# Gated attention with a low-rank mixer: rank sums in four parts, the 64-row tile's products on column halves, the opening's panels in order of use

## The chip, the cores and the metric

The kernel runs on one core of a Trainium2 chip. The metric is the device time of one execution in microseconds. Before the change the median of 11 runs is 1012.69 us (1009.78 to 1018.38).

## The reference

There are 8 batches of 3136 rows. Attention comes first, without a softmax; then a mixer, which adds a low-rank mix over the rows and a two-layer product over the channels:

```
scores = (z @ z.T) / 3136            # z: 3136 x 64; scores are symmetric
x      = u * (max(scores, 0)**2 @ v) # u, v: 3136 x 256
h      = (x.T @ U) @ V               # U: 3136 x 32, V: 32 x 3136
y      = x + h.T
out    = y + max(y @ w_ch1, 0) @ w_ch2   # 256 -> 1024 -> 256
```

Inputs and output are float32; the kernel multiplies in bf16 and sums in float32.

## The kernel before, in words

The rows are cut into 25 tiles: 24 of 128 rows (row index p*24 + t, so a tile is a stride over the rows) and tile 24, called NF, of 64 rows. The tiles are taken in the order 12, 13, ..., 24, 0, ..., 11 (`turns`). NT is 25, FIRST is 12, LEAD is 16, NG is 4.

**Scores.** Row panel j of the squared scores lies in A[j] and covers tiles j to j+12 (cyclically), 13 blocks of 128 columns. `score` (L298) makes a piece with two matmuls over 64 rows, one in each row half of the array; ScalarE applies ReLU and scale out of PSUM (L311), VectorE squares in place (L313). Scores are symmetric, so the blocks that tile o needs from the other 12 panels are the transpose of its own panel: SyncE's queue sends a DMA transpose into a strip (`turn`, L333). There are five strip buffers. `block` gives either a piece of A or of a strip.

**Attention.** `attend_steps` sums, for output tile o, 25 blocks of scores times v. Each block is split in two row halves (`half`, L371), which go to two PSUM banks; tiles go in pairs that share the two banks. `close_pair` adds the halves (ScalarE copy L385, VectorE add L386) and multiplies by u (L395), which gives x. Tile NF uses quarters (`quarter`, L405). There are two sets of two banks; `spare()` is the set that the open pair doesn't hold, or the one closed last where no pair is open. The scores of later panels are strewn between the attention's matmuls by `_spread`; the tables `own_at`, `first_at` and `next_at` say in which turn i of the loop each panel is made, and `turn(b, turns(i + AHEAD))` at the end of a turn transposes four tiles ahead.

**Mixer.** It lags a batch behind. `rank` (L462) sums x.T @ U over the tiles with U as the 32-column stationary operand, in all four 32-column groups of the array; every tile's product is made twice, so that groups 0 and 1 together hold the sum, and groups 2 and 3 hold it again. ScalarE casts the 128x256 result to t1_sb (L472). `low_rank` (L508, L522) multiplies by V over 64 rows and adds into x; then a DMA transpose (L481) makes ut. Chunks c of up to four tiles follow: `up_steps` (L540, ReLU in L558) makes the first products, `down_steps` (L582, L593) the second, adds x and stores. They run as bursts after turns 4, 8, 13 and 17, two chunks in each. Chunk 3 holds tiles NF, 0 and 1. First and second products of neighbouring chunks are interleaved evenly by `_merge`. With `alone`, every second step of first products uses the spare banks and splits its ReLU between VectorE and ScalarE; that is so for chunk 0.

**The end.** After the last batch's attention there come the last rank sum, in two parts with what is left of the batch before (the list `late`), then the last batch's own bursts with its low-rank products in them.

**The opening.** `start_up` computes tiles 12 to 15 with early scores, then tiles 16 to 19 from panels that are finished meanwhile: `rest` holds the missing parts of panels 8 to 15 (one block for panel 8, eight for panel 15), `more` the whole panels 20 to 23. Early loads go through GpSimd's queue, among them the first parts of the next batch's v. A tiny DMA into `mark` on SyncE's queue waits for the last of these parts, and so holds the first DMA transposes back until the loads have landed. The loop proper begins at turn 8, which is tile 20.

All engines follow the order in which the program is written out (the schedule is by hand), each with its own queue.

Of the kernel before, what the change touches and what calls it, by code (L numbers as in the profile page):

```python
# [7 lines left out]
FP32 = mybir.dt.float32  # L8
# [34 lines left out]
def kernel(  # L43
# [56 lines left out]
    def spare():  # L100

        return sets[(opened[0] + (0 if acc else 1)) % 2]
# [29 lines left out]
    def turns(i):  # L132
        return (FIRST + i) % NT
# [24 lines left out]
    def x_at(b, t, n=1):  # L158

        c, k = offset[t]  # L160
        return group(b, c)[:, :, k : k + n, :].rearrange("p a t c -> p t a c")
# [153 lines left out]
    def score_steps(b, j, k0=0, k1=NB):  # L315
        steps = []
        n = (k1 - k0) * P
        parts = _ceil_div(n, 1024)
        each = n // parts
        h = each // 2  # L320
        for i in range(parts):
            at = k0 * P + i * each

            def step(at=at):
                dst = A[j][:, at : at + each].rearrange("p (i h) -> p i h", i=2)
                score(b, [(j, j * P + at + i * h, h, dst) for i in range(2)])

            steps.append(step)
        return steps
# [124 lines left out]
    def rank(b, ps, n0=0, n1=NT):  # L454
# [17 lines left out]
        nc.scalar.copy(out=t1_sb, in_=ps[:, :D])  # L472
        t1[b] = t1_sb

    uT = {}

    def turn_x(b, c):
# [86 lines left out]
    def down_steps(b, c):  # L564
        pairs = []
        for t in chunks[c]:
            if pair_of(t)[0] == t:
                pairs.append([])
            pairs[-1].append(t)
        at = {}  # L570
        for t in chunks[c]:
            at[t] = sum(P if k < NF else TAIL for k in at)
        hold = {}

        def step(n, k):
            pair = pairs[n]
            if k == 0:
                hold[0] = spare()[1 - n]
            ps = hold[0]
            q = at[pair[k]]  # L580
            for ht in range(NH):
                mm(  # L582
                    out=ps[:, k * D : (k + 1) * D],
                    lhsT=relus[c][:, ht, q : q + P],
                    rhs=w2_bf[:, ht, :],
                    start=(ht == 0),
                    stop=(ht == NH - 1),
                )
            if k == len(pair) - 1:
                t, nk = pair[0], len(pair)  # L590
                o_sb = out_pool.tile([P, 2, D], FP32, name="o_sb")
                p = P if t < NF else TAIL
                nc.vector.tensor_tensor(  # L593
                    out=o_sb[:p, :nk, :].rearrange("p t (a c) -> p t a c", c=P),
                    in0=split(ps[:p, : nk * D]),
                    in1=x_at(b, t, nk)[:p],
                    op=ALU.add,
                )
                store = pool_dma if b + 1 < B else nc.sync.dma_start
                if t < NF:  # L600
                    store(out=rows(out[b])[:, t : t + nk, :], in_=o_sb[:, :nk, :])  # L601
                else:
                    store(out=out[b, NF * P :, :], in_=o_sb[:TAIL, 0, :])

        return [
            lambda n=n, k=k: step(n, k) for n in range(len(pairs)) for k in range(len(pairs[n]))
        ]

    def bursts_of(b):

        out_ = []
        for c in range(NC + 1):
            up = [lambda s=s, c=c: up_steps(c, c == 0)[s]() for s in range(NH // 2)] if c < NC else []
            down = down_steps(b, c - 1) if c else []
            out_.append((up, down))
        return out_
# [10 lines left out]
    def start_up():  # L627
# [26 lines left out]
            load_z(1, WHOLE)  # L654
        run(fetches)
        if B > 1:
            for part in V_PARTS[:4]:
                load_v(1, part)
        nxt = [s for j in range(LEAD, LEAD + NG) for s in turned(0, j)]
        rooms = [A[j % NT][:, : 2 * NG * P] for j in range(LEAD + NG, LEAD + 3 * NG)]  # L660
# [27 lines left out]
        for i, pair in enumerate(pairs):  # L688
            if i == 5 and B > 1:

                nc.sync.dma_start(out=mark, in_=v_both[1][:1, V_PARTS[3][1] - 1, :8])
            if i == 3:
                double_z(0, parts[2:])
            if i == 5:
                turn_on_pe([(16, NF)], [pair_psum().rearrange("p a w -> p (a w)")])
                turn_on_pe([(NF, NT)], [pair_psum()[:, 0, :]])
                extend_z(0)
            make(pair)
            if i > 5 and i % 2:
                nxt.pop(0)()  # L700
            if i > 1:
                use(pairs[i - 2], outs)
# [33 lines left out]
        ]  # L736
        run(_merge(nxt[2:], own))
        rest = []
        for j in range(FIRST - NG, LEAD):
            rest += score_steps(0, j, LEAD + NG - j, NB)  # L740
        more = [s for j in range(LEAD + NG, LEAD + 2 * NG) for s in score_steps(0, j)]
        for i, pair in enumerate(pairs):
            if i + 2 < len(pairs):
                make_stored(pairs[i + 2])
# [10 lines left out]
        for o in outs:  # L755
            js = [(o + 1 + i) % NT for i in range(HALF)]

            def close(o=o, j=js[-1]):
                beside(o, j, block(0, o, j), [o % 2 == 1] * 2)
                if o % 2:  # L760
                    close_pair(0, o)
                if o == outs[1]:
                    load_u(0, LEAD + NG)
                if o < outs[-1]:
                    turn(0, o + NG + 1)

            for i in range(3):
                some = js[4 * i : min(4 * i + 4, HALF - 1)]
                tail.append(lambda o=o, js=some: [beside(o, j, block(0, o, j)) for j in js])
            tail.append(close)  # L770
# [8 lines left out]
    for j, i in enumerate((6, 7, 8, 9, 3, 5, 4, 2, 9, 8, 7, 6)):  # L779
        own_at[i].append((j, 0, FIRST - j))  # L780

    first_at = {8: [(NT - 1, 0, NB), (0, 0, NB)], 9: [(1, 0, NB)], 10: [(2, 0, NB)]}
    first_at.update({11: [], 12: []})
    for j, i in zip(range(3, FIRST), (9, 10, 11, 11, 11, 12, 12, 12, 12)):
        first_at[i].append((j, 0, FIRST - j))

    next_at = {i: [] for i in range(NT)}
    for j in range(FIRST):
# [12 lines left out]
    for b in range(B):  # L801
        more = b + 1 < B
        begin = 0 if b else 2 * NG
        bursts = bursts_of(b - 1) if b else []
        burst_at = {4: (0, 1), 8: (2, 3), 13: (4, 5), 17: (6, 7)}
        own = own_at if b else first_at
        v_at = dict(zip((9, 12, 15, 18, 21), V_PARTS[4:]))
        ahead = dict(zip((2, 3, 6, 7, 10, 11, 14), range(NC)))
        for i in range(begin, NT):
            o = turns(i)  # L810
            fill = [s for key in own.get(i, ()) for s in score_steps(b, *key)]
            if more:
                fill += [s for key in next_at[i] for s in score_steps(b + 1, *key)]
                if b and i == 1:
                    load_z(b + 1, WHOLE)
                if b and i == 7:
                    turn_z(b + 1, ((FIRST, NF),))
                if b and i == 10:
                    turn_z(b + 1, ((0, FIRST),))
                if b == 0 and i in v_at:  # L820
                    load_v(b + 1, v_at[i])
                if i == 11:
                    extend_z(b + 1)
            main = attend_steps(b, o)
            if b and i in ahead:
                main.insert(17 if (i + (i > FIRST)) % 2 == 0 else 10, lambda c=ahead[i]: low_rank(b - 1, c))
            _spread(main, fill)
            if i + AHEAD < NT:
                turn(b, turns(i + AHEAD))
            elif more:  # L830
                turn(b + 1, turns(i + AHEAD - NT))
            elif i == NT - AHEAD:
                turn_x(b, 0)
            if b == 0 and i in puts:
                puts[i]()
            if b and i == 0:
                rank(b - 1, spare()[0])
            for n in burst_at.get(i, ()) if b else ():
                up, down = bursts[n]
                if not more and n >= NC - 1:  # L840
                    late += up + (down if n == NC else [])
                    up, down = [], (down if n < NC else [])
                steps = _merge(up, down)
                if more:
                    loads = [lambda k=k: load_v(b + 1, V_PARTS[k]) for k in ((n,) if n < NC else (n, n + 1))]
                    steps = _merge(steps, loads)
                    if n == 1:
                        for k, part in ((6, (FIRST, NF)), (3, (0, FIRST))):
                            steps.insert(k, lambda part=part: double_z(b + 1, (part,)))
                run(steps)  # L850
# [14 lines left out]
    for c in range(NC + 1):  # L865
        up, down = last[c]
        if c + 2 < NC:
            up.insert(3 if c == 0 else 1, lambda c=c: low_rank(b, c + 2, other))
        if c == 0:
            up.insert(1, lambda: low_rank(b, 0, other, False))  # L870
        run(_merge(up, down))

# [28 lines left out]
```

## Time and profile before

| | |
|---|---|
| median of 11 runs | 1012.69 us (1009.78 to 1018.38) |
| profiled execution | 1018.05 us, span 1016.3 us |
| TensorE busy | 992.1 us, 13823 matmuls |
| rank sums (L462) | 400 matmuls, 13.0 us |
| second products (L582) | 1600 matmuls, 204.7 us |
| granted TensorE clock | 0.998 |

Busy time is the union of an engine's instructions. A matmul's own duration includes its way through the array, and neighbours overlap; so what a group of matmuls costs is read from the start of the group to the start of the next. "Idle before, releaser" tells how long an engine waited before an instruction and what ended the wait.

### The profile page before, as it was taken

The numbers are of one execution on the slowest core, as the hardware profiler recorded it, in microseconds if no ns is written. First come the engines' busy times: TensorE is split into PE (matmuls) and PEld (weight loads), VectorE is DVE, ScalarE is ACT, GpSimd is POOL, SyncE is SP. The second block draws the span as 40 slices with busy tenths as digits, with TensorE's granted clock in tenths as the row PEclk, the third lists the DMA queues.
The fourth block names the chain that finished last, engine by engine and source line by source line (L and its number), as shares of the span: only waits on it lengthen the run. The fifth ranks groups of instructions, "written<-read, shape, count | busy, mean of one in ns | idle before, by whom it ended". The sixth has DMA issues, their size and how long they took to land.

```text
span 1016.3 us, 31322 instructions
## 1 busy us (share of the span) xinstructions
PE 992.1 (98%) x13823; PEld 784.9 (77%) x13863; DVE 540.0 (53%) x978; ACT 614.3 (60%) x835; POOL 171.7 (17%) x317
## 2 busy tenths in 40 slices
PE   8899999999999999899999999999999999999998
PEld 6678777887778877688787887778877788787866
DVE  6877654465445564346644556445664356542242
ACT  7977764576646675356764667556674666643154
POOL 5111112111121111121112211112111120011000
PEclk9999999999999999999999999999999999999999
DMA  9999989899898989989989999999989998667442
GB/s 186 198 212 184 181 130 206 170 175 156 184 170 168 184 152 150 172 170 174 162 174 168 182 167 147 186 167 172 174 153 194 167 184 143 141 145 168 105 97 95
DMA packets 414648, 167.97 MB, mean 165 GB/s; under 512 B 389472, under 2 KB 399136, under 8 KB 414512
## 3 DMA queue, kind: packets, MB, share of 16 engines
q1 hardware_dynamic: 385280, 99.68, 62.2%
q0 software_dynamic: 29232, 66.28, 28.2%
q8 instruction: 108, 1.77, 0.7%
q14 instruction: 28, 0.23, 0.1%
HBM read 61.88 MB, written 25.69 MB: 86 GB/s over the span
## 4 chain that ended last, share of the span: by engine, by line
PE 85%; DMA 6%; DVE 4%; ACT 2%; issue 1%; POOL 1%; SPq 0%; DVEq 0%; POOLq 0%; ACTq 0%
PE ps L371 44%; PE ps L582 16%; PE ps L540 16%; PE ps L298 6%; ACT A L311 2%; DMA strip<-A 2%; DMA out_dram<-o_sb 2%; DVE A L313 1%; PE ps L405 1%; PE ps L462 1%; DVE x_bf L522 1%; PE ps L508 1%; DMA z_c<-in_z_dram 1%; DMA ut<-x_bf 1%; DVE both L386 1%
## 5 line engine op out<-in xcount | busy, mean ns | idle before, releaser
L311 ACT ACTIVATE A<-ps 128x832 bf16<-128x832 f32 (+8 forms) x477 | 359.8, 769 | 153.0 <-PE ps L298 145.2
L371 PE MATMUL ps<-v,A 64*128 64x256 bf16 x4988 | 341.8, 269 | 4.6 <-DVE A L313 2.3
L313 DVE TENSOR_TENSOR A<-A 128x832 bf16<-128x832 bf16 (+8 forms) x477 | 244.9, 526 | 145.1 <-ACT A L311 141.8
L371 PE MATMUL ps<-v,strip 64*128 64x256 bf16 x4420 | 307.0, 269 | 1.4 <-DMA strip<-A 1.4
L371 PEld LDWEIGHTS <-A 64*128 64x128 bf16 x4988 | 244.8, 94 | 49.9 <-issue 14.0
L558 ACT ACTIVATE relu_bf<-ps 128x1024 bf16<-128x1024 f32 (+2 forms) x208 | 187.8, 909 | 143.6 <-PE ps L540 141.5
L371 PEld LDWEIGHTS <-strip 64*128 64x128 bf16 x4420 | 221.2, 94 | 36.0 <-DMA strip<-A 2.2
L593 DVE TENSOR_TENSOR o_sb<-ps,x_bf 128x512 f32<-128x512 f32 (+1 forms) x104 | 69.7, 670 | 254.5 <-PE ps L582 232.4
L582 PE MATMUL ps<-w_bf,relu_bf 128*128 128x256 bf16 x1600 | 204.7, 273 | 0.0
L540 PE MATMUL ps<-ut,w_bf 128*128 128x512 bf16 (+2 forms) x856 | 197.3, 351 | 3.5 <-DMA ut<-x_bf 1.0
L582 PEld LDWEIGHTS <-relu_bf 128*128 128x128 bf16 x1600 | 155.9, 98 | 47.0 <-issue 2.9
L540 PEld LDWEIGHTS <-w_bf 128*128 128x128 bf16 x896 | 85.0, 98 | 62.5 <-issue 6.2
L355 POOL DMA_DIRECT2D u_sb<-in_u_dram x96 | 53.6, 558 | 464.1 <-DVE x_bf L395 431.8
L298 PE MATMUL ps<-zT 64*128 64x416 bf16 (+8 forms) x812 | 130.7, 312 | 0.0
L385 ACT COPY both<-ps 128x512 f32<-128x512 f32 (+1 forms) x104 | 58.9, 566 | 80.8 <-PE ps L371 68.4
L601 POOL DMA_DIRECT2D out_dram<-o_sb x84 | 46.0, 548 | 278.1 <-DVE o_sb L593 274.7
L386 DVE TENSOR_TENSOR both<-ps,both 128x512 f32<-128x512 f32 (+1 forms) x104 | 69.2, 666 | 28.8 <-ACT both L385 28.5
L395 DVE TENSOR_TENSOR x_bf<-both,u_sb 128x512 bf16<-128x512 f32 (+1 forms) x104 | 69.8, 671 | 3.6
L522 DVE TENSOR_TENSOR x_bf<-ps,x_bf 128x512 bf16<-128x512 f32 (+1 forms) x112 | 65.4, 625 | 8.7 <-PE ps L508 8.7
L298 PEld LDWEIGHTS <-zT 64*128 64x128 bf16 x812 | 42.2, 94 | 4.0
L244 POOL DMA_DIRECT2D v<-in_v_dram x61 | 34.1, 561 | 2.0 <-DMA w_bf<-in_moe_w_ch_dram 1.0
L298 PE MATMUL ps<-relu_bf 64*128 64x416 bf16 (+9 forms) x121 | 21.9, 332 | 3.2 <-ACT A L311 2.5
(49 smaller groups left out, 209.6 us busy)
## 6 DMA issues: line engine op xcount, KB each, us to landing
u_sb<-in_u_dram POOLq DMA_DIRECT2D x96, 256.0 KB, 3.7
out_dram<-o_sb POOLq DMA_DIRECT2D x84, 256.0 KB, 3.1
v<-in_v_dram POOLq DMA_DIRECT2D x57, 192.0 KB, 4.7
strip<-A SPq DMA_TRANSPOSE x196, 5.5
out_dram<-o_sb SPq DMA_DIRECT2D x12, 256.0 KB, 2.0
z_c<-in_z_dram POOLq DMA_DIRECT2D x7, 384.0 KB, 5.5
u_sb<-in_u_dram POOLq DMA_DIRECT2D x16, 64.0 KB, 2.4
ut<-x_bf SPq DMA_TRANSPOSE x56, 3.5
```

Of the source, the lines that this page charges most:

```text
L298: mm(out=ps[:, k, :n], lhsT=zT[halves[k], j, :], rhs=zT_flat[halves[k], c : c + n], start=True, stop=True,)
L311: nc.scalar.activation(out=dst, in_=src, func=AF.Relu, scale=sc)
L313: nc.vector.tensor_tensor(out=dst, in0=dst, in1=dst, op=ALU.mult)
L371: mm(out=acc[t0][h][:, (o - t0) * D : (o - t0 + 1) * D], lhsT=w[halves[h]], rhs=v_both[b % 2][halves[h], j, :], start=start, stop=stop, **kw,)
L385: nc.scalar.copy(out=both[:, :w], in_=banks[1][:, :w])
L386: nc.vector.tensor_tensor(out=both[:, :w], in0=banks[0][:, :w], in1=both[:, :w], op=ALU.add)
L395: nc.vector.tensor_tensor(out=x_at(b, t0, n), in0=split(both[:, :w]), in1=u_sb[:, :n, :].rearrange("p t (a c) -> p t a c", c=P), op=ALU.mult,)
L522: nc.vector.tensor_tensor(out=q, in0=split(ps[h][:, : len(ks) * D]), in1=q, op=ALU.add)
L540: mm(out=ps[i][:, :w] if apart else ps[:, i, :w], lhsT=w1_bf[:, db, (hp + i) * P : (hp + i + 1) * P], rhs=uT[c][:, db, len(chunks[c]) * P ...
L558: nc.scalar.activation(out=relus[c][:, hp : hp + 2, :w], in_=ps[:, :, :w], func=AF.Relu)
L582: mm(out=ps[:, k * D : (k + 1) * D], lhsT=relus[c][:, ht, q : q + P], rhs=w2_bf[:, ht, :], start=(ht == 0), stop=(ht == NH - 1),)
L593: nc.vector.tensor_tensor(out=o_sb[:p, :nk, :].rearrange("p t (a c) -> p t a c", c=P), in0=split(ps[:p, : nk * D]), in1=x_at(b, t, nk)[:p] ...
```

## The change

The rank sum of batches 0 to 6 is formed once: every tile's product goes into one of four column groups in turn, so that each group holds a quarter of the sum. ScalarE copies the four parts to a float32 buffer, and VectorE adds the two row halves crosswise, so that both halves hold the same pair of sums as before. The last batch keeps `rank`.

The second products of tile NF use 64 columns instead of a 128-column window of which half was not used; the eight blocks of the sum alternate between the array's column halves, and VectorE adds the two results. In the bursts this tile's second product is taken first, ahead of the interleaving.

In the opening, the panels 15 to 8 of `rest` come in descending order; panel 23 is made in turn 8, and the panels of tiles 24, 1, 2 and 3 each a turn later than before, with those of 4 to 11 partly moved as well; the transposes of tiles 23, 24 and 0 follow in turns 8 and 9. Three parts of v instead of four are loaded early, and `mark` waits for the third.

At the end, chunk 6 of the batch before the last is also treated as `alone`, and the last batch's first low-rank product takes the set of banks that `spare()` gives.

```diff
+    def rank_once(b, ps):
+        for m in range(NT):
+            g = m % G
+            mm(
+                out=ps[g * R : (g + 1) * R, :D],
+                lhsT=U_bf[:, turns(m), :],
+                rhs=x_at(b, turns(m))[:, 0],
+                start=(m < G),
+                stop=(m + G >= NT),
+            )
+        t1_sb = small.tile([P, D], BF16, name="t1_sb")
+        sums = both_pool.tile([P, 512], FP32, name="both")
+        nc.scalar.copy(out=sums[:, :D], in_=ps[:, :D])
+        for h in range(2):
+            nc.vector.tensor_tensor(
+                out=t1_sb[halves[h], :],
+                in0=ps[halves[h], :D],
+                in1=sums[halves[1 - h], :D],
+                op=ALU.add,
+            )
+        t1[b] = t1_sb
...
             for ht in range(NH):
+                two = pair[k] == NF
+                r = halves[ht % 2] if two else slice(0, P)
                 mm(
-                    out=ps[:, k * D : (k + 1) * D],
-                    lhsT=relus[c][:, ht, q : q + P],
+                    out=ps[r, k * D : (k + 1) * D],
+                    lhsT=relus[c][:, ht, q : q + (TAIL if two else P)],
                     rhs=w2_bf[:, ht, :],
-                    start=(ht == 0),
-                    stop=(ht == NH - 1),
+                    start=(ht < 1 + two),
+                    stop=(ht >= NH - 1 - two),
                 )
...
+                if t == NF:
+                    o_flat = o_sb[:TAIL, 0, :]
+                    nc.vector.tensor_tensor(
+                        out=o_flat, in0=ps[halves[1], :D], in1=o_flat, op=ALU.add
+                    )
...
-            up = [lambda s=s, c=c: up_steps(c, c == 0)[s]() for s in range(NH // 2)] if c < NC else []
+            alone = c == 0 or (c == NC - 1 and b == B - 2)
+            up = [lambda s=s, c=c, a=alone: up_steps(c, a)[s]() for s in range(NH // 2)]
+            up = up if c < NC else []
...
-            for part in V_PARTS[:4]:
+            for part in V_PARTS[:3]:
...
-                nc.sync.dma_start(out=mark, in_=v_both[1][:1, V_PARTS[3][1] - 1, :8])
+                nc.sync.dma_start(out=mark, in_=v_both[1][:1, V_PARTS[2][1] - 1, :8])
...
-        for j in range(FIRST - NG, LEAD):
+        for j in reversed(range(FIRST - NG, LEAD)):
             rest += score_steps(0, j, LEAD + NG - j, NB)
-        more = [s for j in range(LEAD + NG, LEAD + 2 * NG) for s in score_steps(0, j)]
+        more = [s for j in range(LEAD + NG, LEAD + 2 * NG - 1) for s in score_steps(0, j)]
...
-                if o < outs[-1]:
+                if o < outs[-2]:
                     turn(0, o + NG + 1)
...
-    first_at = {8: [(NT - 1, 0, NB), (0, 0, NB)], 9: [(1, 0, NB)], 10: [(2, 0, NB)]}
-    first_at.update({11: [], 12: []})
-    for j, i in zip(range(3, FIRST), (9, 10, 11, 11, 11, 12, 12, 12, 12)):
+    first_at = {8: [(NT - 2, 0, NB), (0, 0, NB)], 9: [(NT - 1, 0, NB)], 10: [(1, 0, NB)]}
+    first_at.update({11: [(2, 0, NB)], 12: []})
+    for j, i in zip(range(3, FIRST), (10, 11, 11, 12, 12, 12, 12, 12, 12)):
         first_at[i].append((j, 0, FIRST - j))
+    first_turns = {8: (NT - 2,), 9: (NT - 1, 0)}
...
-        v_at = dict(zip((9, 12, 15, 18, 21), V_PARTS[4:]))
+        v_at = dict(zip((9, 11, 13, 15, 18, 21), V_PARTS[3:]))
...
-            if i + AHEAD < NT:
+            if b == 0 and i in first_turns:
+                for t in first_turns[i]:
+                    turn(b, t)
+            elif i + AHEAD < NT:
                 turn(b, turns(i + AHEAD))
...
-                rank(b - 1, spare()[0])
+                rank_once(b - 1, spare()[0])
...
-                steps = _merge(up, down)
+                steps = [down.pop(0)] if n == 4 else []
+                steps += _merge(up, down)
...
-            up.insert(1, lambda: low_rank(b, 0, other, False))
+            up.insert(1, lambda: low_rank(b, 0, None, False))
```

## The prediction

> **What bounds the kernel now.** I read the page first: engine shares, DMA queues, then the chain that ended last.
>
> ```profile
> PE 992.1 (98%) x13823; PEld 784.9 (77%) x13863; DVE 540.0 (53%) x978; ACT 614.3 (60%) x835; POOL 171.7 (17%) x317
> q1 hardware_dynamic: 385280, 99.68, 62.2%
> q0 software_dynamic: 29232, 66.28, 28.2%
> PE 85%; DMA 6%; DVE 4%; ACT 2%; issue 1%; POOL 1%; SPq 0%; DVEq 0%; POOLq 0%; ACTq 0%
> ```
>
> TensorE is never long idle, and the chain runs on it. A matmul removed there is time removed, unless something else is nearly as full: the two data queues together hold 62.2 + 28.2 = 90.4% of the DMA engines' time, which I come back to. DVE (53%) and ACT (60%) have room for small additions.
>
> A matmul's mean of 273 ns is latency; the price is the distance from one group's start to the next group's start. So I read TensorE's timeline: the first rows are around one rank sum in the middle (batch 0's was at 104 us, this is the next), the others are the end of the kernel. Columns: start, length, engine, line, count, and in brackets the idle time before and its releaser.
>
> ```profile
> 227.89 1.60 PE L462 MATMUL ps<-x_bf,U_bf 128*32 128x256 bf16 x50
> 229.43 0.94 PE L371 MATMUL ps<-v,A 64*128 64x256 bf16 x14
> ...
> 958.91 1.39 PE L462 MATMUL ps<-x_bf,U_bf 128*32 128x256 bf16 x44
> 960.23 1.05 PE L540 MATMUL ps<-ut,w_bf 128*128 128x256 bf16 x8
> 961.59 1.09 PE L540 MATMUL ps<-ut,w_bf 128*128 128x256 bf16 x8 [0.31 <-ACT relu_bf L558]
> 962.60 0.40 PE L462 MATMUL ps<-x_bf,U_bf 128*32 128x256 bf16 x6
> 962.93 1.05 PE L582 MATMUL ps<-w_bf,relu_bf 128*128 128x256 bf16 x8
> 963.91 0.39 PE L492 MATMUL ps<-V_bf,t_sb 64*128 64x512 bf16 x2
> ```
>
> 50 rank matmuls hold TensorE for 229.43 - 227.89 = 1.54 us, 44 for 1.32, 6 for 0.33. Counted in rounds of four (13, 11, 2) all three fit 0.11 us a round plus 0.11 us for leaving the shape: four 32-column products go through together in the time of one. A full-width second product pays 0.11 each: (963.91 - 962.93)/8 = 0.12 with the change of shape in it.
>
> **Rank sums.** 50 matmuls become 25 for seven batches (the last keeps the old form): 7 rounds for 13, so 6 x 0.11 = 0.66 us each, **7 x 0.66 = 4.6 us**. The cast on ACT becomes a copy of the same 128x256 (0.37 us). Two 64x256 adds on DVE are new; the nearest row is the 128x256 sum of L386 at 0.42 us, so 0.84 us. Their bank is next opened two tiles later and t1_sb is first used then too: a tile takes about 4 us, so copy and adds (1.2 us) are hidden; without that cover they would cost up to 1.2 x 7 = 8.4 us. Behind the adds on DVE waits the square of the next tile's score, whose own ACT pass is not over before the adds are.
>
> **64-row tile.** Eight 128-column products become eight 64-column ones that alternate between column halves. No row shows 128 rows by 64 columns. Bounds: no overlap, 8 x 0.11 = 0.88 us, nothing won; full overlap, four rounds, 0.44. The nearest rows are the rank's (128*32, four at once) and the 64*64 tail of the attention (49 in 1.53 us, about four at once): full overlap. The Trainium skill speaks against this: "TensorEngine Tiling (Array Packing)", Gotcha 2 (Feature Incompatibilities), says that column tiling excludes the fast weight load. Here are the weight loads of full columns, of 32 and of 64:
>
> ```profile
> L582 PEld LDWEIGHTS <-relu_bf 128*128 128x128 bf16 x1600 | 155.9, 98 | 47.0 <-issue 2.9
> L462 PEld LDWEIGHTS <-U_bf 128*32 128x32 bf16 x400 | 10.3, 96 | 2.1 <-issue 1.9
> L405 PEld LDWEIGHTS <-strip 64*64 64x64 bf16 x192 | 6.2, 115 | 0.1
> ```
>
> By the rule loads would get longer; "TensorE: Matmul & The Clock Gate", Weight-path perf modes, puts the fast load at about twice the rate. A doubled 98 ns, one after another, would make 8 x 0.196 = 1.6 us and the tile 0.7 us slower (an estimate from that page). The rows show 96 and 115 ns beside 98, and several loads within one round, so I take the rows. Gain 8 x 0.44 = 3.5 us. Against it stands a change of shape: the same rows give 0.10 us for one. Taking the tile's product first in its burst puts it directly behind attention, which changed shape there anyway, so one is added, not two; in the last batch one too, as a low-rank product (another shape) follows it. 8 x 0.10 = 0.8. **Net 2.7 us.** The new 64x256 add (0.42 us, DVE) lies before a store that nobody waits for soon.
>
> **Opening.** Three rows of TensorE, then SP's queue and POOL's v loads.
>
> ```profile
> 47.91 0.72 PE L371 MATMUL ps<-v,A 64*128 64x256 bf16 x10 [1.19 <-DVE A L313]
> 49.50 0.50 PE L371 MATMUL ps<-v,strip 64*128 64x256 bf16 x6 [0.36 <-DMA strip<-A]
> 58.46 0.28 PE L371 MATMUL ps<-v,strip 64*128 64x256 bf16 x1 [0.62 <-DMA strip<-A]
> ...
> 30.74 0.82 SPq L691 DMA_DIRECT2D mark<-v  x1
> 31.61 7.82 SPq L333 DMA_TRANSPOSE strip<-A  x4
> ...
> 22.51 0.53 POOL L244 DMA_DIRECT2D v<-in_v_dram  x1 [1.01 <-DMA w_bf<-in_moe_w_ch_dram]
> 23.73 0.53 POOL L244 DMA_DIRECT2D v<-in_v_dram  x1 [0.69 <-DMA U_bf<-in_moe_U_dram]
> ```
>
> The 1.19 us wait is for the square of the last and largest rest panel; the new order makes it first, and two 832-wide ACT passes (0.77 us each) leave this stretch, so it goes. But what is late next is the strip awaited at 49.50: SP runs without a gap from the mark on, and the mark waits for v's last early part. With three parts instead of four the mark can go about 1.0 us sooner (the issues are 1.22 us apart), and every strip with it. So TensorE leads by that 1.0 us, not by 2.2. Against it: the panels of the last two tiles are now scored a turn or more later and their transposes stand in SP's one queue, behind them those of tiles 0, 1 and on. Tile 24's panel is ready about 3 us after SP would be free for it; its strip and tile 0's then come near the moment they are wanted (62 and 65 us). The v part moved into the main loop also adds its DMA (192 KB) there, and the next parts come two turns apart instead of three on POOL; u loads behind it are delayed 0.55 us an issue. Bounds: +1.5 us of new strip waits net; -2.2 us if all three waits above (1.19 + 0.36 + 0.62) go. I take **-1.0**, the SP row.
>
> **End.** The late first products use the other banks alternately: the second group of 8 should have begun at 960.23 + 0.88 = 961.11 and began at 961.59; of this 0.48 about 0.1 stays (ACT still has half of each second step), gain 0.4. The first low-rank product moves to the other set and no longer waits for DVE (about 0.9 us), but the next first product needs that set: DVE empties the earlier product until 967.37 and the moved one's banks at 968.0 and 968.65 (0.64 us each), so it ends near 969.1, before at 967.72 + 0.86 = 968.6: a loss of 0.5. Together **0.0**, between -0.5 and +0.5.
>
> **Sum.** 4.6 + 2.7 + 1.0 + 0.0 = 8.3 us. The profiled execution took 1018.05 us (span 1016.3, 1.75 around it), so this one with the same stalls would take 1009.7. It lies 5.4 us above the median of 1012.69; the views of waits show why:
>
> ```profile
> DVE zT L238 <- DMA zT<-z_bf: 6.6, 3, 4.8
> PE ps L405 <- DVE x_bf L522: 4.3, 3, 3.6
> PE ps L371 <- DVE o_sb L593: 2.1, 2, 1.3
> ```
>
> These are single stalls in two or three batches, which come and go; the change takes none of them away on purpose. From the median: 1012.69 - 8.3 = **1004.4 us**.
>
> **Rivals.** (a) The column halves don't overlap: the 3.5 us are missing, 1007.9 us. For it: only the skill's rule; against it: the rows. (b) The opening loses instead of winning, by late strips of tiles 23 to 0: +1.5 instead of -1.0, 1006.9 us. For it: SP without gaps; against it: strips after 60 us were not awaited. (c) DMA takes the gain: a batch shorter by 1 us asks for the same transfers, and stores and strips come later by as much: 1012 us, no change. For it: 90%; against it: in most batches TensorE waits for no DMA at all. (d) Slower: the copy that extends zT (L238) stands in DVE's queue in front of the low-rank evictions, and waits for a transpose sent only one tile before. Where that took long (4.83 us in one batch) TensorE lost 3.6 + 1.3 = 4.9 us. If earlier arrival made this happen in more batches, two would eat the gain (8.3/4.9 = 1.7) and three give 1012.7 - 8.3 + 14.7 = 1019 us. Against it: nothing between that transpose and that copy is changed.
>
> **How the numbers follow.** Main 0.55, (a) 0.08, (b) 0.20, (c) 0.10, (d) 0.07. About 0.3% (3 us) is what a measurement of this kernel can tell from no change; main, (a) and (b) lie beyond it: faster 0.83, same 0.10, slower 0.07. The main case's own range is 1001.5 to 1007 (opening -2.2 to 0, end 0.5 either way, and some stalls more or less in the median); (a) and (b) take it to 1009. (c) and (d), 0.17, are left out; the lower end is 1000.5 for an opening in which every wait goes and fewer stalls.
>
> **What would show it.** Rank groups of 25 that hold TensorE for 0.88 us; eight 64-column products in about 0.44 us plus 0.10; the wait for DVE near 47 us gone, and the first strip wait still there, 1 us earlier; the batch period near 121.4 us instead of 122.4 (rank sums at 227.96 and 350.37 in the chain by time) where no stall falls in. Wrong would be: 64-column products at 0.11 us each, strip waits of over 1 us between 55 and 67 us, or DVE's wait before L238 of some us in most batches.

## The result, and the profile after

The changed kernel takes 1005.5 us (median of 12 runs, 1003.6 to 1009.41). The runs of the kernel before, taken with it and earlier, have a median of 1013.54 us. The ratio is 0.9918 with a 95% interval of 0.9899 to 0.9936: about 8.3 us faster by the ratio (8.0 by the two medians), where 8.3 were forecast, and 1005.5 us where 1004.4 were. The sum was right, but in part by luck: one of its terms had the wrong sign, and something outside the sum made up for it, as the following shows. Each ratio below is to runs of the kernel before that were taken beside it (medians 1012.51 to 1013.38 us).

From the page of the changed kernel (its profiled execution took 1005.05 us):

```profile
span 1003.3 us, 30977 instructions
PE 984.2 (98%) x13648; PEld 776.7 (77%) x13688; DVE 550.5 (55%) x1002; ACT 612.3 (61%) x835; POOL 171.7 (17%) x317
q1 hardware_dynamic: 385280, 99.68, 61.9%
q0 software_dynamic: 29232, 66.28, 28.2%
```

175 matmuls fewer, nothing else about the balance has moved: TensorE is still the bound, and the DMA queues carry the same bytes.

TensorE's timeline of the changed kernel: one rank sum, then the 64-row tile's second products between attention and the next first products.

```profile
228.11 0.94 PE L479 MATMUL ps<-x_bf,U_bf 128*32 128x256 bf16 x25
228.98 0.94 PE L371 MATMUL ps<-v,A 64*128 64x256 bf16 x14
...
170.94 0.63 PE L608 MATMUL ps<-w_bf,relu_bf 128*64 128x256 bf16 x8
171.50 1.04 PE L563 MATMUL ps<-ut,w_bf 128*128 128x512 bf16 x3
```

The rank sum holds TensorE for 228.98 - 228.11 = 0.87 us instead of 1.54, the eight 64-column products for 0.56 us with their change of shape. Their weight loads, in the groups by shape:

```profile
L608 PEld LDWEIGHTS <-relu_bf 128*128 128x128 bf16 x1536 | 149.7, 98 | 44.4 <-issue 2.7 <-ACT relu_bf L581 0.2
L608 PEld LDWEIGHTS <-relu_bf 128*64 128x64 bf16 x64 | 2.9, 109 | 1.9 <-issue 1.9
```

A load of 64 columns takes 109 ns instead of 98, and two lie beside each other: 64 loads cover 2.9 us, 45 ns each (1536 loads of full columns cover 149.7 us, 97 ns each).

The opening, on TensorE and on SP's queue:

```profile
46.83 0.53 PE L371 MATMUL ps<-v,A 64*128 64x256 bf16 x6
49.70 0.50 PE L371 MATMUL ps<-v,strip 64*128 64x256 bf16 x6 [2.34 <-DMA strip<-A]
...
30.17 0.81 SPq L724 DMA_DIRECT2D mark<-v  x1
31.04 8.90 SPq L333 DMA_TRANSPOSE strip<-A  x4
40.05 3.35 SPq L195 DMA_TRANSPOSE zT<-z_bf  x2
```

The wait for VectorE near 47 us is gone, as forecast, but the wait for tile 20's strip ends at 49.70, not at 48.5: before, it ended at 49.50. In this pair of profiles the mark started 0.57 us earlier and the strip came no earlier.

To set the pieces apart I use three distances in each profile. They are the start of the first rank sum (everything in the opening lies ahead of it), the distance from one rank sum to the next (a batch; the smallest value recurs to 0.01 us, for the kernel before over several profiles with the same main loop, and I call it the clean period), and the distance from the last rank sum to the end of the span.

| kernel | first rank sum, us | clean period | last rank sum to end | median, us |
|---|---|---|---|---|
| before | 104.37 | 122.25 | 57.40 | 1013.54 |
| changed | 106.90 | 121.21 | 57.36 | 1005.50 |
| rank sums alone | 105.50 | 121.52 | 57.41 | 1006.38 |
| 64-row tile alone | 105.94 | 121.92 | 57.09 | 1012.40 |
| opening alone | 106.02 | 122.24 | 57.41 | 1013.42 |
| changed, old opening | 105.37 | 121.20 | 57.35 | 1003.25 |
| changed, old opening, old low-rank place | 103.83 | 121.20 | 56.92 | 1001.13 |

### The profile page after: what moved, and what is told of

It is laid out like the page before. It is cut to its first block, busy times and chain, and to the rows that moved or that the text cites. A ratio compares the mean times of both kernels' runs of the same rounds, so it can differ in the third digit from the quotient of the medians.

```text
span 1003.3 us, 30977 instructions
## 1 busy us (share of the span) xinstructions
PE 984.2 (98%) x13648; PEld 776.7 (77%) x13688; DVE 550.5 (55%) x1002; ACT 612.3 (61%) x835; POOL 171.7 (17%) x317
## 4 chain that ended last, share of the span: by engine, by line
PE 89%; DVE 4%; DMA 3%; ACT 3%; issue 1%; POOL 0%; DVEq 0%; ACTq 0%; POOLq 0%
PE ps L371 46%; PE ps L608 17%; PE ps L563 17%; PE ps L298 6%; ACT A L311 3%; DVE A L313 1%; DVE x_bf L545 1%; PE ps L405 1%; DMA strip<-A 1%; PE ps L531 1%; DMA zT<-z_bf 1%; DMA z_c<-in_z_dram 1%; PE ps L479 1%; DVE both L386 1%; DVE x_bf L395 0%
## 5 line engine op out<-in xcount | busy, mean ns | idle before, releaser
L311 ACT ACTIVATE A<-ps 128x832 bf16<-128x832 f32 (+9 forms) x477 | 359.0, 769 | 156.0 <-PE ps L298 150.1
L313 DVE TENSOR_TENSOR A<-A 128x832 bf16<-128x832 bf16 (+9 forms) x477 | 244.5, 526 | 133.5 <-ACT A L311 130.4
L608 PE MATMUL ps<-w_bf,relu_bf 128*128 128x256 bf16 (+1 forms) x1600 | 201.5, 273 | 0.2 <-ACT relu_bf L579 0.2
L608 PEld LDWEIGHTS <-relu_bf 128*128 128x128 bf16 (+1 forms) x1600 | 152.6, 98 | 46.3 <-issue 4.6
L563 PEld LDWEIGHTS <-w_bf 128*128 128x128 bf16 x896 | 85.2, 98 | 63.2 <-issue 7.3
```

The lines of the kernel that those rows point to most:

```text
L311: nc.scalar.activation(out=dst, in_=src, func=AF.Relu, scale=sc)
L313: nc.vector.tensor_tensor(out=dst, in0=dst, in1=dst, op=ALU.mult)
L563: mm(out=ps[i][:, :w] if apart else ps[:, i, :w], lhsT=w1_bf[:, db, (hp + i) * P : (hp + i + 1) * P], rhs=uT[c][:, db, len(chunks[c]) * P ...
L608: mm(out=ps[r, k * D : (k + 1) * D], lhsT=relus[c][:, ht, q : q + (TAIL if two else P)], rhs=w2_bf[:, ht, :], start=(ht < 1 + two), stop=( ...
```

## The experiments

**Everything but the opening.** All the opening's edits are undone, from the order of the panels to the parts of v; for example

```diff
-            for part in V_PARTS[:3]:
+            for part in V_PARTS[:4]:
...
-        for j in reversed(range(FIRST - NG, LEAD)):
+        for j in range(FIRST - NG, LEAD):
...
-        more = [s for j in range(LEAD + NG, LEAD + 2 * NG - 1) for s in score_steps(0, j)]
+        more = [s for j in range(LEAD + NG, LEAD + 2 * NG) for s in score_steps(0, j)]
```

> All of the change except the opening, which is as before. If the opening costs 2.5 us (clock theory: the wait for tile 20's strip grew to 2.3 us and the granted clock then fell to 0.50 for 3.3 us), the first rank sum starts near 104.4 us instead of 106.9, and the kernel takes about 1003.0 us (changed kernel 1005.5). If the opening is worth the 1.0 us of the prediction, it takes about 1006.5 and the first rank sum starts near 107.9.

Measured: 1003.25 us (6 runs, 1000.5 to 1009.61), ratio to before 0.9899 [0.9858, 0.9940]; the first rank sum at 105.37. The interval holds the changed kernel's 0.9918, so the times alone do not settle it; the median and the profile both point to an opening that costs, not to one that is worth 1.0 us.

**The opening alone**, the same edits put into the kernel before.

> The kernel before with the new opening alone. Clock theory: the wait for tile 20's strip is over 2 us, the clock falls to 0.50 behind it, the first rank sum starts near 106.9 us instead of 104.4, and the time is 2 to 3 us above the kernel before. By the prediction's own step it is 1.0 us faster. If the opening's moved loads are what took stalls out of later batches, the batches after it are free of them and the time is at or below that of before.

Measured: 1013.42 us (12 runs), ratio 1.0001 [0.9975, 1.0027], the first rank sum at 106.02. No gain. The mark started at 28.95 us and tile 20's strip landed at 48.77, both the earliest of all the profiles; TensorE still lost 2.9 us at it, and the granted clock fell to 0.50 for a while behind it, as in the changed kernel. Stalls in batches 1, 3 and 5 were there as before (periods of 123.82, 123.22 and 123.64).

**Rank sums alone**: `rank_once` in the kernel before, as in the change.

> The kernel before with rank sums formed once, nothing else. By the prediction each of seven sums holds TensorE for 0.88 us instead of 1.54, 4.6 us less in all: about 1008.5 us, with a batch period of 121.75 us where no stall falls in. Rival, DMA takes the gain: the period stays at 122.4 us and waits for strips or stores grow by as much.

Measured: 1006.38 us (7 runs), ratio 0.9923 [0.9895, 0.9952], so 4.9 to 10.6 us; clean period 121.52. The period shrinks by 0.73 us, a little more than the 0.66 of the matmuls; no wait grows by as much, so DMA does not take the gain.

**The 64-row tile alone**: the second products of tile NF on column halves, first in their burst.

> The kernel before with the 64-row tile's second products on column halves, taken first in their burst. By the prediction 0.34 us a batch, 2.7 us in all: about 1010.5 us, the eight products held for 0.55 us with the change of shape, a period of 122.05 us. Rival, the halves don't overlap: 0.98 us for the eight, no gain.

Measured: the eight products hold TensorE for 0.56 us, the clean period is 121.92 (0.33 less), and the last rank sum lies 0.31 us nearer to the end. So the halves overlap. The median is 1012.40 us, ratio 0.9991 [0.9965, 1.0016]: the interval reaches to 3.5 us faster and so holds the 2.7 us of the forecast, but also no gain at all. The profile shows the gain; the runs neither confirm nor contradict it.

**The tile's product back among the first products** of its burst, in the changed kernel:

```diff
-                steps = [down.pop(0)] if n == 4 else []
-                steps += _merge(up, down)
+                steps = _merge(up, down)
```

> The changed kernel with the 64-row tile's product back in its place between first products. By the prediction one more change of shape, 0.10 us a batch: a clean period of 121.3 us instead of 121.2. If the first place was what mattered, for instance by covering a wait, the period grows by 0.3 us or more.

One run: 1006.52 us, clean period 121.31 instead of 121.21. So one change of shape is 0.10 us; the timeline of this kernel shows where it is paid.

```profile
172.81 1.04 PE L563 MATMUL ps<-ut,w_bf 128*128 128x512 bf16 x4
173.78 0.63 PE L608 MATMUL ps<-w_bf,relu_bf 128*64 128x256 bf16 x8
174.34 1.04 PE L563 MATMUL ps<-ut,w_bf 128*128 128x512 bf16 x4
```

173.78 - 172.81 = 0.97 us for four matmuls that take 0.87 (175.21 - 174.34) where the shape does not change behind them.

**The clock.** In the changed kernel the granted clock fell 1.3 us after the strip's wait had ended. A table by stretch, two of the changed kernel and then one of the kernel before; the columns are the length of the stretch, busy time and count of PE, PEld, DVE, ACT and POOL, then the granted clock, the DMA share and GB/s:

```profile
49.70:51.00 1.30, 1.30 (x22) 1.08 (x24) 0.00 (x0) 0.58 (x1) 0.00 (x0) 1.00 1.20 198
51.00:54.30 3.30, 3.30 (x34) 2.26 (x30) 1.19 (x2) 1.64 (x3) 0.00 (x0) 0.50 1.10 148
```

```profile
51.00:54.30 3.30, 3.30 (x64) 2.80 (x60) 2.36 (x5) 3.17 (x5) 0.00 (x0) 1.00 0.92 161
```

34 matmuls went through in 3.3 us where the kernel before put 64 through in the same stretch. I took this for the cause of the opening's loss and filled the wait with 18 useless matmuls:

```diff
+            if b == 0 and i == 8:
+                main.insert(13, keep_busy)   # 18 x 128x256 into a PSUM tile that nobody reads
             _spread(main, fill)
```

> The changed kernel with 18 useless matmuls (about 2.0 us, into a PSUM tile that nobody reads) where tile 20's first strip is awaited. Clock theory: the wait stays, TensorE is busy in it, the granted clock stays 1.00 in the 6 us after it, and the first rank sum starts about 1.5 us earlier than the 106.9 of the changed kernel, near 105.4. Rival, the loss is the work moved behind the strip and the strips' lateness alone: the first rank sum stays near 106.9 or comes later.

The clock stayed at 1.00 and the first rank sum came at 105.83, as the clock theory has it; but the opening alone had reached its own at 106.02 with the slow clock, and the median is 1005.61 us (10 runs), the changed kernel's own. Then the changed kernel itself was profiled again:

> The changed kernel once more, unaltered, to see whether its opening repeats. Clock theory: the wait for tile 20's strip is over 2 us again; where it passes about 2.5 us the granted clock falls to 0.50 for some 3 us right after it, and where it stays near 2.1 us (as in the run with the tile's product merged) it may hold. That strip lands between 49.1 and 49.9 us whatever the mark does.

```profile
49.86 0.50 PE L371 MATMUL ps<-v,strip 64*128 64x256 bf16 x6 [2.35 <-DMA strip<-A]
56.94 0.50 PE L371 MATMUL ps<-v,strip 64*128 64x256 bf16 x6 [0.50 <-DMA strip<-A]
59.66 0.28 PE L371 MATMUL ps<-v,strip 64*128 64x256 bf16 x1 [1.00 <-DMA strip<-A]
```

The same wait of 2.35 us, this time without a fall of the clock (1.00 in every stretch from 50 to 56 us), and the first rank sum came even later, at 107.33: TensorE ran at full speed into later strips. It lost 0.7 us before the group at 56.94 and 1.2 us before the one at 59.66 (the brackets hold the idle part of it). So the theory falls as the cause: the slow clock made TensorE late at strips that would have kept it waiting as well. Nor does the length of the wait decide alone: with the tile's product among the first products 2.15 us were lost at tile 20's strip, and the clock stayed at 1.00.

**The mark alone**: three early parts of v, mark on the third, panels in the old order.

> The kernel before with three early parts of v instead of four and the mark on the third, panels in the old order. By the prediction's step tile 20's strip lands 1.0 us earlier, near 48.5 us instead of 49.5. If the transposes run at the rate of the DMA engines rather than of the queue, the mark goes up to 1 us earlier and that strip still lands within 0.4 us of 49.5.

One run: 1013.05 us. The mark started at 29.67, and tile 20's strip landed at 49.29 (before: 30.74 and 49.45). Over the fourteen profiles of this study the mark's start spreads over 2.4 us (28.95 to 31.34) and the landing of that strip over 1.1 us (48.77 to 49.89); a straight line through them gives about 0.4 us of landing for 1 us of mark, and the landing belonging to the latest mark is 49.51, in the middle. With the scatter this large, one pair of profiles says little; the means say more. In the six profiles with three early parts the mark starts at 29.98 us and the strip lands at 49.38, in the eight with four at 30.43 and 49.51: 0.45 us and 0.14 us sooner, with a scatter of about 0.5 us and 0.4 us. The issues on SP's queue follow each other without a gap, but they grow longer where they start earlier: the first four transposes took 9.04 us behind the mark at 29.67, 7.82 behind that at 30.74 and 7.45 behind that at 31.34. That SP's queue was full did not mean that an earlier start would be passed on to its end; what the issues then wait for was not tested.

**The order alone**: only the rest panels in descending order.

> The kernel before with the rest panels 15 to 8 in descending order and nothing else; panel 23 stays where it was. The 1.19 us wait for the square of panel 15 is gone. If the strip sets the time, the wait for tile 20's strip grows by about that and the first rank sum stays within 0.5 us of the old opening's (104.4 to 105.9 in four profiles). If the strip's wait stays near 1.5 us, the clock stays 1.00; if it passes 2 us, it falls as in the changed kernel.

Measured: 1013.13 us (10 runs), ratio 0.9991 [0.9966, 1.0016]; the first rank sum at 105.68. The wait for VectorE is gone, and the distance lost ahead of tile 20's strip is 1.96 us instead of 0.58: the 1.40 us that the other wait had cost, to 0.02. The clock stayed at 1.00 there.

**Padded rank sums.** The kernel with the new rank sums alone, each sum followed by the same 25 matmuls once more into a bank that nobody reads.

```diff
+        for m in range(NT):
+            g = m % G
+            mm(
+                out=pad[g * R : (g + 1) * R, :D],
+                lhsT=U_bf[:, turns(m), :],
+                rhs=x_at(b, turns(m))[:, 0],
+                start=(m < G),
+                stop=(m + G >= NT),
+            )
```

> Rank sums formed once, as in the kernel with that part alone, followed by 25 matmuls of the same shape into the set's other bank, which nobody reads. If the saved matmul time is the whole gain, a clean period goes back to 122.2 us or slightly above and the median to within 1.5 us of the kernel before. If the new copy and adds, or something else than the time on TensorE, took the stalls of batches 1, 3 and 5 away, these stalls stay away and the median is 2 us or more below the kernel before.

Measured: 1014.30 us (10 runs), ratio 1.0020 [0.9994, 1.0045], clean period 122.29. With TensorE's time given back, the whole gain is gone: it was those matmuls, and the new copy and adds cost next to nothing.

**The end, and a better version.** Old opening, and the last batch's first low-rank product back on its old banks:

```diff
-            up.insert(1, lambda: low_rank(b, 0, None, False))
+            up.insert(1, lambda: low_rank(b, 0, other, False))
```

> The change without its opening and without the moved first low-rank product of the last batch; the late first products stay on alternate banks. The wait of 1.2 us behind the moved product goes and the two waits of 0.33 and 0.49 us come back: from the last rank sum to the end about 57.0 us instead of 57.36, and the median near 1003, within 1 us of the run with the old opening.

Measured: 1001.13 us (4 runs, 1000.5 to 1002.8), ratio 0.9886 [0.9870, 0.9903]; from the last rank sum to the end 56.92 us. The low-rank product's place in the change cost 0.44 us, which the timelines show. First the changed kernel, then this one:

```profile
953.47 0.39 PE L531 MATMUL ps<-t_sb,V_bf 64*128 64x256 bf16 x4
954.91 0.59 PE L563 MATMUL ps<-ut,w_bf 128*128 128x512 bf16 x2 [1.04 <-DVE x_bf L545]
```

```profile
949.54 0.27 PE L531 MATMUL ps<-t_sb,V_bf 64*128 64x256 bf16 x1 [0.17 <-DVE x_bf L545]
950.14 0.38 PE L531 MATMUL ps<-t_sb,V_bf 64*128 64x256 bf16 x3 [0.33 <-DVE x_bf L545]
950.44 1.90 PE L563 MATMUL ps<-ut,w_bf 128*128 128x512 bf16 x8
```

Two short waits are exchanged for one that is longer than both. This is the best version of the study.

**Filling the strip's wait with useful work.** In that version, the order of use and panel 24 scored before the strip is awaited:

```diff
-        for j in range(FIRST - NG, LEAD):
+        for j in reversed(range(FIRST - NG, LEAD)):
...
-        more = [s for j in range(LEAD + NG, LEAD + 2 * NG) for s in score_steps(0, j)]
+        more = [s for j in range(LEAD + NG, NT) for s in score_steps(0, j)]
...
-    first_at = {8: [(NT - 1, 0, NB), (0, 0, NB)], 9: [(1, 0, NB)], 10: [(2, 0, NB)]}
+    first_at = {8: [(0, 0, NB)], 9: [(1, 0, NB)], 10: [(2, 0, NB)]}
```

> The same with the rest panels in descending order and panel 24 scored before tile 20's strip is awaited, instead of in turn 8. As the strip lands near 49.5 us anyway, this puts about 0.7 us of TensorE's and 1.5 us of ScalarE's work into a wait: the wait for the strip falls from about 2.0 us to near 1.0, and the first rank sum starts 0.5 to 0.7 us earlier than with the old opening, unless the strips of later tiles are what comes late next; then it starts as before.

Measured: 1003.17 us (6 runs), ratio 0.9913 [0.9889, 0.9937]; the first rank sum at 104.89, within the range of the old opening. The wait for tile 20's strip is gone from the profile, but TensorE then waits 0.70 us for VectorE at 50.40 and 0.24 us for a strip at 58.92. It gained nothing.

## Why the prediction was right, and where it was not

**Rank sums: right.** 0.87 us a sum against 0.88, and 5.1 us by the period over seven batches (7 x 0.73) against 4.6. That the copy and the two adds are hidden holds: the padded kernel has them too and lies at the kernel before.

**64-row tile: right by the profiles,** though the runs alone could not tell it from no gain. 0.56 us for the eight against 0.54; 0.33 us a batch against 0.34; one change of shape is 0.10 us. The loads of 64 columns, which spoke against it, are 11 ns longer (109 against 98), and two overlap; no row tells whether the 98 ns are those of a fast weight load.

**Opening: wrong in sign.** The step that failed is "with three parts instead of four the mark can go about 1.0 us sooner, and every strip with it". Both halves of it were too large. Over the profiles with three early parts the mark went 0.45 us sooner in the mean, and tile 20's strip 0.14 us; against the kernel before, the strip landed 0.2 us later in the changed kernel, 0.16 us earlier with the mark alone and 0.68 us earlier with the opening alone. "What is late next is the strip" was right, as the order alone shows to 0.02 us, but moving the strip was worth a few tenths of a microsecond at most, too little to tell from the scatter, not 1.0. The upper bound of +1.5 us, meant for late strips, was reached by something else. Turn 12 is the 64-row tile; its products have another shape than scores, so every score piece there costs two changes of shape. The change moves two more pieces into it. The first profile line is of the kernel before, the second of the changed one: scores of that turn, in the groups by line. The third is the wait that stands in the second, from the timeline.

```profile
L298 PE MATMUL ps<-relu_bf 64*128 64x256 bf16 (+3 forms) x8 | 1.0, 239 | 0.0
```

```profile
L298 PE MATMUL ps<-relu_bf 64*128 64x384 bf16 (+5 forms) x12 | 1.6, 263 | 0.6 <-ACT A L311 0.5
64.94 0.29 PE L298 MATMUL ps<-relu_bf 64*128 64x256 bf16 x2 [0.54 <-ACT A L311]
```

That turn takes 4.23 us instead of 2.73, in all five profiles of the new opening (4.22 or 4.23) and in none of the nine others (2.73 or 2.74): 1.5 us. Of these 0.54 us are a wait for ScalarE, whose passes over the scores take 4.8 us in that turn where they took 2.4; the rest is the two pieces with their changes of shape. Ahead of the turn old and new arrive alike, at 61.2 to 62.9 us in six profiles with the old opening and 61.7 to 63.2 in four with the new (the one with the filled wait is left aside); behind it the distance to the first rank sum is the same 39.86 us in eight of these ten (two with the old opening have 40.84 and 41.20). The first rank sum starts at 104.98 us in the mean of those six and at 106.51 in the mean of the four. Single profiles scatter by as much as these means differ, so the 1.5 us rest on the turn, which repeats to 0.01 us. So the opening cost 1.5 us, 2.5 us off the forecast; the medians with the opening alone neither show nor exclude that. Rival (b) is what happened, with another mechanism than late strips. That the turn is the whole of it is read from these distances; a new opening with its table for turn 12 alone undone was not tried.

**End: nearly right.** Forecast 0.0. The tile's share of 0.31 us lies in the end too, so the 57.36 us of the changed kernel are 0.27 us above the 57.09 of the tile alone. The late first products are worth 0.17 us (57.09 against 56.92) instead of 0.4: behind them the second product waits 0.2 us for their last ReLU, which the sum left out. The moved low-rank product costs 0.44, against 0.5.

**The sum.** Clean terms as measured: 7 x 1.04 (122.25 - 121.21) + 0.31 - 0.27 - 1.5 = 5.8 us, while the runs show 8.3 (interval 6.5 to 10.2). The kernel's fastest runs moved by 5.4 us (1009.02 to 1003.6). What is missing in between are stalls that come and go. Summed over the six periods between the first rank sum and the seventh, the time above the clean period was 10.0, 4.1, 2.7, 3.7 and 6.2 us in the five profiles with the old rank sum, and 0.7 to 3.8 us in the eight with the new one (the 10.0 are of an execution 4.5 us above the median). The prediction left these stalls as they were; they became fewer, which made good for the opening. That the whole forecast hit is thus luck: two errors of about 2.5 us that cancel. The padded kernel says what the stalls go with. Its one profile shows only 1.8 us of them, but that execution was the fastest of its ten (1010.71 us). By the medians it is 7.9 us slower than the new rank sums alone (1014.30 against 1006.38), of which the period explains 7 x 0.77 = 5.4: with TensorE's time about 2.5 us of stalls came back as well, though the new copy and adds were still there. Why a batch shorter by 0.7 us has fewer of them is not settled. Rivals (c) and (d), more waiting for DMA, are not what happened on the whole: the kernel gained, and the views of waits of the two profiles show less of it, not more.

```profile
DVE zT L238 <- DMA zT<-z_bf: 3.5, 3, 1.6
PE ps L405 <- DVE x_bf L545: 1.1, 3, 0.4
```

Before, these were 6.6 us and 4.3 us.

## What to carry to other kernels

Price a group of small matmuls by the distance to the next group's start, in rounds that share the array, plus one change of shape; both terms held here to 0.02 us. When a wait is taken away, look for the arrival that comes next and ask what sets its time: a queue that issues without gaps need not pass an earlier start on (here 0.14 us of 0.45). Work moved out of a crowded stretch is not free where it lands: count the changes of shape and ScalarE's time in the turn that receives it.

## What the runs showed of the hardware

A TensorE wait of 2.34 us was followed, 1.3 us after its end, by a granted clock of 0.50 for about 3.3 us in one profile, and one of 2.35 us by nothing in another of the same kernel. The Trainium skill, "TensorE: Matmul & The Clock Gate", Part 1 (The HAM clock gate), says that the gate watches activity in a window that runs free of the program; the two profiles agree with that, though no run here shows the window itself.

The two column halves of a 128-row product overlapped fully: eight 256-wide products in 0.56 us, with about 0.10 us of it for the change of shape.
